# Masks by ScalarE, one product with U per batch, and u's transposes through one queue: a fused attention and low-rank mixing kernel on one core

## The chip, the core and the metric

The kernel runs on one core of a Trainium2 chip. The core has five engines that run in parallel, each with its own in-order queue and joined by semaphores: TensorE (PE in the profile; its weight loads are PEld), VectorE (DVE), ScalarE (ACT), GpSimd (POOL) and SyncE (SP), which here only issues transfers. PE writes to PSUM, where VectorE and ScalarE read its results. The metric is the time of one execution on the device in microseconds; a lower time is better. All times below are microseconds unless marked ns.

## The reference

Eight batches, eight heads, 576 positions, head width 64. Heads 0 to 3 attend locally (a position sees itself and the 31 before it), heads 4 to 7 in strides of 32. Then a mixing step over positions of rank 32, and a two-layer channel network with a residual.

```
rel = pos[:, None] - pos[None, :]
mask_local = (rel >= 0) & (rel < 32)
mask_strided = (rel >= 0) & (pos[None, :] % 32 == pos[:, None] % 32)
scores = np.where(masks, q @ k.T / 8, -1e9)
attn = exp(scores - max); attn /= sum + 1e-9
x = concat over heads of attn @ v          # 8 x 576 x 512
h = x.T @ U @ V                            # U 576 x 32, V 32 x 576
u = x + h.T
out = u + relu(u @ w_ch1) @ w_ch2          # 512 -> 2048 -> 512
```

The two weights arrive as 64-bit floats and are turned into 32-bit parts on the core.

## The kernel before

The channel network makes up most of the work. It runs over blocks of 512 rows: block n (0 to 7) holds the first 512 positions of batch n, and block 8 the last 64 positions of all eight batches. Each block has 16 steps `fc`, one for each 128 of the 2048 hidden columns. `gemm1` (L648) is 12 matmuls into one PSUM bank `ph`: four pieces `dc` of u^T, each as three products of a high and a low part (`uh`, `ul`, and the weights' two parts). ScalarE makes the hidden value `gh` of it (L652), VectorE its low part `gl` (L653). `gemm2` (L665) is 12 matmuls into the two accumulators `acc`. The main loop at the end of the function issues `gemm1` of a step, then `gemm2` of the step before. At the end of a block, `finish` adds the accumulator to u (L672) and sends it out, and `split` (L637) makes `uh` and `ul` of the next block from `raw`, which holds u^T.

The attention of a batch runs beside the block before its own. `attention(b)` is a generator; `advance` runs a number of its steps in each of the 32 slots of a block, two slots per step of the network, by the triple `A_EARLY` (block 0), `A_LATE` (blocks 1 to 6) or `A_TAIL`: first slot, last slot, number of steps. Its order for batches 2 to 7:

- `local_pairs`: two pairs of local heads. Per pair: PSUM tile `px` is taken (`psx2`; there is one, of two banks, and every stage below takes it in turn); two matmuls with an identity write the mask into it (L340, bfloat16, 320 columns for each head); 72 small matmuls add the scores (L346); VectorE takes the maximum and subtracts, ScalarE the exponential (L361); PE transposes (L368), ScalarE copies to `PT` (L371); 80 small matmuls with V (L381); VectorE normalises (L390 to L397).
- `mix_t`, first half of the columns, then the copies of the strided heads' result (`strided_copies`, L487 and L491), then `mix_t`, second half. `mix_t` is U^T x: four matmuls over four groups of 128 positions, each to its own 32 partitions (L514), four more for the last 64 positions (L518), whose results are added up by a copy on ScalarE (L523) and three adds on VectorE (L525), and made into three stacked parts `tst` (L527 to L529).
- `mix_u` and `mix_tail`: V's product (L537, L546) and its addition to x (L539, L552).
- `transposes`: VectorE transposes blocks of 32 by 32 into `bt` (L619), and 16 transfers per half, by SP and ScalarE in turn, move these into `raw`, in runs of 512 bytes.

The strided heads of batches 2 to 7 are done by GpSimd and VectorE without PE: `strided_heads` has GpSimd multiply (L442 for the scores, L470 for the values) and VectorE sum (L444, L472). `strided_upto` paces its 66 steps between the slots that `S0` and `S1` give, about from the middle of one block into the next.

Batches 0 and 1 are done by `first_attention`, ahead of the first block and into its first steps, with all their heads on PE; batch 1's mixing runs in block 0, with `attention(1)`, beside the conversion of the remaining weights (`to_f32` L129 to L132, `weights` L205 and L206).

The order of the instructions in each engine's queue is not the order in which the code writes them down. A scheduler takes it from a model of the times and from the order of the code as priority. `tc.issue_after(ins)` adds an edge: what the block writes comes behind `ins` in the queue of `ins`'s engine. `marks` collects instructions for such edges.

Of the kernel before, what the change touches and what calls it, by code (L numbers as in the profile page):

```python
# [17 lines left out]
NSP = 2  # L18
N_EARLY = 20
N_LATE = 48  # L20
N_STRIDED = 66
# [16 lines left out]
def fused_kernel(ctx, tc, pairs, strided, U, V, w_in, masks, eye, out):  # L38
    nc = tc.nc
    B, S, DM = out.shape  # L40
    D = 64
# [72 lines left out]
    zeros = raw.rearrange("p s a d x -> p (s a d x)")[:, 0:320].bitcast(BF16)  # L114
    nc.vector.memset(zeros, 0.0)
# [215 lines left out]

    def scores(kT, qT, mask):

        sp = psx2()
        done = marks.setdefault("scores", [])
        with tc.issue_after(done[-1]) if len(done) == 1 else nullcontext():
            for n in range(WARM.get(len(done), 0)):
                nc.tensor.matmul(sp[:, 0, :], zeros[:, 0:128], zeros[:, 128:640], start=True, stop=True, skip_group_check=True)
        for hh in range(2):
            nc.tensor.matmul(sp[:, hh, 0:320], ident_b, mask, start=True, stop=False, skip_group_check=True)  # L340
        for c in range(NCH):
            t, c4 = c // 4, c % 4
            k0 = max(0, 32 * c - 32)
            x0 = 64 * t + (0 if c else 32)
            for hh, rows in enumerate(halves):
                last = nc.tensor.matmul(sp[32 * c4:32 * c4 + 32, hh, x0:64 * t + 64], qT[rows, 32 * c:32 * c + 32],  # L346
                                        kT[rows, k0:32 * c + 32], start=False, stop=True, skip_group_check=True,
                                        tile_position=(64 * hh, 32 * c4))
        done.append(last.ins)
        return sp[:, :, 0:320].rearrange("p h (t x) -> p h t x", x=64)  # L350
# [23 lines left out]
    def outputs(PT, vt):  # L374

        op = psx2()
        for c in range(NCH):
            t, c4 = c // 4, c % 4
            for o4 in (c4,) if t < 4 else (c4, c4 + 2):
                for hh, rows in enumerate(halves):  # L380
                    last = nc.tensor.matmul(op[32 * o4:32 * o4 + 32, hh, (D + 1) * t:(D + 1) * t + D + 1],  # L381
                                            PT[rows, 32 * c:32 * c + 32], vt[rows, c], start=True, stop=True,
                                            skip_group_check=True, tile_position=(64 * hh, 32 * o4))
        marks.setdefault("PV", []).append(last.ins)
        return op[:, :, 0:5 * (D + 1)].rearrange("p h (t x) -> p h t x", x=D + 1)
# [15 lines left out]
    def local_pairs(b):  # L401

        xg, xt = x_tiles(b)
        tb = 64 * (b % 2)
        for pr in range(2):
            kT, qT = load_qk(b, pr)
            vt = load_v(b, pr)
            for _ in range(2):
                yield
            sp = scores(kT, qT, mask_l)  # L410
            yield
            s_sb = yield from probabilities(sp)
            yield
            PT = transposed(s_sb)
            yield
            op = outputs(PT, vt)
            yield
            cs = slice(2 * pr * D, 2 * pr * D + 2 * D)
            normalised(op, xg[:, :, cs], xt[tb:tb + 64, cs], tb)
            yield  # L420

    def strided_heads(b):
# [15 lines left out]
        for i in range(NCH):  # L438
            for j0 in range(0, i + 1, 9):
                n = min(9, i + 1 - j0)  # L440
                tmp = att([128, 9, D], "tmp")
                nc.gpsimd.tensor_tensor(out=tmp[:, 0:n], in0=sk[:, j0:j0 + n], in1=sq[:, i:i + 1].broadcast_to([128, n, D]),  # L442
                                        op=ALU.mult)
                late.append(lambda tmp=tmp, n=n, i=i, j0=j0: nc.vector.tensor_reduce(  # L444
                    out=s_st[:, i, j0:j0 + n], in_=tmp[:, 0:n], axis=AX.X, op=ALU.add))
                flush(1)
                yield
# [17 lines left out]
        for i in range(NCH):  # L465
            step = D if i < 9 else D // 2
            for d0 in range(0, D, step):
# [3 lines left out]
                                        in1=s_st[:, i, 0:i + 1].broadcast_to([128, i + 1, step]), op=ALU.mult)  # L471
                late.append(lambda tv=tv, i=i, d0=d0, step=step: nc.vector.tensor_reduce(  # L472
                    out=o_st[:, i, d0:d0 + step], in_=tv.rearrange("p j d -> p d j"), axis=AX.X, op=ALU.add))
# [28 lines left out]

    def mix_t(b, half):

        xg, xt = x_tiles(b)
        tb = 64 * (b % 2)
        cs = slice(256 * half, 256 * half + 256)
        ps_a = psx1()[:, 0:256]
        if b not in tsts:
            tsts[b] = ap_.tile([96, DM], F32R, name="tst")  # L510
        tst = tsts[b]
        with tc.issue_after(marks["acc"][2 + half]) if b < NSP else nullcontext():
            for j in range(4):
                nc.tensor.matmul(ps_a[32 * j:32 * j + 32, :], U_sb[:, j, :], xg[:, j, cs], start=True, stop=False,  # L514
                                 skip_group_check=True, tile_position=(0, 32 * j))
        for j in range(4):
            part = slice(64 * j, 64 * j + 64)
            nc.tensor.matmul(ps_a[32 * j:32 * j + 32, part], U_sb[tb:tb + 64, 4, :],  # L518
                             xt[tb:tb + 64, 256 * half + 64 * j:256 * half + 64 * j + 64], start=False, stop=True,
                             skip_group_check=True, tile_position=(tb, 32 * j))  # L520
        yield
        ta = att([32, 256], "ta")
        nc.scalar.copy(out=ta, in_=ps_a[0:32, :])  # L523
        for j in range(1, 4):
            nc.vector.tensor_tensor(out=ta, in0=ps_a[32 * j:32 * j + 32, :], in1=ta, op=ALU.add)  # L525
        yield
        nc.scalar.copy(out=tst[0:32, cs], in_=ta)  # L527
        nc.scalar.copy(out=tst[64:96, cs], in_=ta)
        nc.vector.tensor_tensor(out=tst[32:64, cs], in0=ta, in1=tst[0:32, cs].bitcast(F32), op=ALU.subtract)  # L529
        yield  # L530
# [64 lines left out]
    def attention(b):  # L595
        if b >= NSP:
            yield from local_pairs(b)
            yield from mix_t(b, 0)
            yield "strided"
            yield from strided_copies(b)  # L600
            yield from mix_t(b, 1)
            yield
# [3 lines left out]
        else:  # L606
            yield from mix_tail(0)
            for half in range(2):
                yield from mix_t(b, half)
            yield from mix_u(b)  # L610
# [3 lines left out]
    def transposes(n):  # L614

        for t in (0, 2):
# [18 lines left out]
    def split(n):  # L635

        for dc in range(NDC):  # L637
            hi, lo = (u[:, dc, :].rearrange("p (s a x) -> p s a x", s=4, a=4) for u in (uh, ul))
            nc.scalar.copy(out=hi, in_=raw[:, :, :, dc, :])  # L639
            nc.vector.tensor_tensor(out=lo, in0=raw[:, :, :, dc, :], in1=hi.bitcast(F32), op=ALU.subtract)  # L640

    accs = {}

    def gemm1(fc, dcs=range(NDC)):
        ph = ps_h.tile([128, 512], F32, name="ph")
        for dc in dcs:
            for i, (part, ut) in enumerate(((0, uh), (0, ul), (1, uh))):
                nc.tensor.matmul(ph, w_parts[fc, 0][:, part, 128 * dc:128 * dc + 128], ut[:, dc, :],  # L648
                                 start=(dc == dcs[0] and i == 0), stop=(dc == dcs[-1] and i == 2))
        gh = mp.tile([128, 512], F32R, name="gh", bufs=2)  # L650
# [18 lines left out]
    def finish(n):  # L669
        for s in range(4):  # L670
            ot = xgs[n][:, s, :]
            nc.vector.tensor_tensor(out=ot, in0=accs[n][s // 2][:, s % 2, :], in1=ot, op=ALU.add)  # L672
            if n == B:
                for bb in range(2):
                    (od_dma if bb else dma)(out=out[2 * s + bb, 512:576, :], in_=ot[64 * bb:64 * bb + 64, :])
            else:
                dma(out=out[n, 128 * s:128 * s + 128, :], in_=ot)

    conv = weights()
# [57 lines left out]
    for step, (n, fc) in enumerate(steps):  # L737
        pend.append((n, fc) + (gemm1(fc, ORDER0) if step == 0 else gemm1(fc)))
        if fc == NFC - 1 and n + 1 < NB:
            split(n + 1)  # L740
        advance(2 * step)
# [86 lines left out]
```

## Time and profile before

| | |
|---|---|
| median of three runs | 927.82 (927.54 to 929.11) |
| the profiled execution | 928.37 |
| its span, first to last instruction | 926.1 |
| granted TensorE clock, mean | 0.991 |
| start of the first `gemm1` | 49.5 |
| DMA, mean over the span | 81 GB/s |

A row of the timeline gives the start, the duration, the engine, line and operation, what it writes and reads, the shape and how many like it follow on each other; in brackets stand the idle time before it and what ended it. A matmul's row lasts longer than the step to the next one, since matmuls overlap; the cost of one in a sequence is read from the starts. A row of the groups ends with the busy time, the mean in ns, and the idle time before. A row of the windows view gives a stretch, its length, the busy time of each engine asked for with its number of instructions, then the granted clock, the share of the DMA engines and GB/s. A row of the waits gives who waited for whom: sum, number, longest.

### The profile page before, as it was taken

The page shows a single profiled execution, that of the slowest core. Times are in us where ns is not written, and L with a number is a line of the kernel's source. Part 1 is how long each engine was busy: PE and PEld are TensorE (multiplying, and loading weights), DVE is VectorE, ACT ScalarE, POOL GpSimd, SP SyncE. Part 2 cuts the span into 40 slices and gives each one's busy share as a digit, 9 for nine tenths or more (in the row PEclk, how much of TensorE's full clock was granted, in tenths as well). Part 3 has the DMA queues.
Part 4 walks back from the last instruction along what each step waited for, and adds up shares of the span by engine and source line. Part 5 has one row for each costly group of instructions (what it writes and reads, how often), then busy time and mean ns, then how long its engine had stood idle before and what let it go on. Part 6 is the DMA issues. An engine that isn't in the chain of part 4 may idle for free.

```text
span 926.1 us, 16819 instructions
## 1 busy us (share of the span) xinstructions
PE 902.6 (97%) x6997; PEld 718.0 (78%) x6998; DVE 548.6 (59%) x895; ACT 244.2 (26%) x478; POOL 338.4 (37%) x378
## 2 busy tenths in 40 slices
PE   7899989999999999999999999999999999999997
PEld 4667767777887788778877787778877888888885
DVE  4579996665886588658765786667863341122111
ACT  3457522142123312331224121422142111121110
POOL 1223493343853393429433764356530000000000
PEclk9899999999999999999999999999999999999999
DMA  9869313201230125011500141014200230001001
GB/s 352 299 205 357 117 54 107 73 2 52 76 145 2 52 55 178 1 52 33 181 8 18 50 168 50 1 53 148 73 1 1 57 120 17 1 1 46 0 1 46
DMA packets 39036, 75.29 MB, mean 81 GB/s; under 512 B 6464, under 2 KB 22864, under 8 KB 37040
## 3 DMA queue, kind: packets, MB, share of 16 engines
q1 hardware_dynamic: 27312, 66.87, 20.7%
q10 hardware_dynamic: 10560, 4.73, 2.0%
q0 software_dynamic: 1088, 2.62, 0.8%
q8 instruction: 55, 0.90, 0.4%
q14 instruction: 21, 0.17, 0.1%
HBM read 54.14 MB, written 11.67 MB: 71 GB/s over the span
## 4 chain that ended last, share of the span: by engine, by line
PE 84%; DVE 4%; DMA 2%; POOL 1%; issue 1%; ACT 0%; SPq 0%; DVEq 0%; ACTq 0%; POOLq 0%
PE acc L665 40%; PE ph L648 39%; PE px L381 1%; DMA w<-in_w_dram 1%; PE px L346 1%; DVE cv L132 1%; DVE s_st L444 1%; PE px L368 1%; PE px L514 1%; DMA od<-x 1%; PE px L537 1%; DMA st<-in_strided_dram 1%; DVE w L206 1%; POOL tmp L442 1%; DVE gl L653 0%
## 5 line engine op out<-in xcount | busy, mean ns | idle before, releaser
L653 DVE SCALAR_TENSOR_TENSOR gl<-ph,gh 128x512 fp32r<-128x512 f32 x144 | 98.9, 688 | 230.1 <-ACT gh L652 229.4
L648 PE MATMUL ph<-uh,w 128*128 128x512 f32 x648 | 215.9, 394 | 0.0
L652 ACT ACTIVATE gh<-ph 128x512 fp32r<-128x512 f32 x144 | 86.2, 599 | 476.9 <-PE ph L648 400.8
L470 POOL TENSOR_TENSOR tmp<-st,s_st 128x448 f32<-128x448 f32 (+7 forms) x162 | 137.3, 876 | 190.8 <-DVE st L472 106.8
L442 POOL TENSOR_TENSOR tmp<-st 128x576 f32<-128x576 f32 (+6 forms) x162 | 175.0, 1121 | 76.5 <-DMA st<-in_strided_dram 66.6
L665 PE MATMUL acc<-w,gh 128*128 128x512 f32 x648 | 196.8, 391 | 0.0
L648 PEld LDWEIGHTS ph<-uh,w 128*128 128x128 f32 x648 | 121.9, 189 | 26.8
L665 PEld LDWEIGHTS acc<-w,gh 128*128 128x128 f32 x648 | 121.3, 188 | 25.6
L472 DVE TENSOR_REDUCE st<-tmp 128x64 f32<-128x64 f32 (+8 forms) x162 | 136.3, 878 | 7.8 <-POOL tmp L470 7.0
L648 PE MATMUL ph<-ul,w 128*128 128x512 f32 x324 | 126.8, 391 | 0.0
L665 PE MATMUL acc<-w,gl 128*128 128x512 f32 x324 | 121.6, 392 | 4.1 <-DVE gl L653 4.1
L444 DVE TENSOR_REDUCE s_st<-tmp 128x9 f32<-128x576 f32 (+6 forms) x162 | 87.2, 563 | 17.5 <-POOL tmp L442 16.7
L665 PEld LDWEIGHTS acc<-w,gl 128*128 128x128 f32 x324 | 61.0, 188 | 18.4 <-DVE gl L653 5.2
L648 PEld LDWEIGHTS ph<-ul,w 128*128 128x128 f32 x324 | 61.1, 189 | 12.6
L487 ACT COPY xg<-st 32x256 f32<-32x256 f32 x96 | 38.8, 404 | 9.1 <-DVE st L472 7.7
L525 DVE TENSOR_TENSOR ta<-px,ta 32x256 f32<-32x256 f32 x42 | 17.6, 420 | 36.5 <-ACT ta L523 35.6
L672 DVE TENSOR_TENSOR xg<-acc,xg 128x512 f32<-128x512 f32 x36 | 22.9, 682 | 13.4 <-PE acc L665 13.4
L539 DVE TENSOR_TENSOR xg<-px,xg 128x512 f32<-128x512 f32 x28 | 18.0, 684 | 11.9 <-PE px L537 11.9
L648 PE MATMUL ph<-uh,w6a 128*128 128x512 f32 x72 | 24.3, 398 | 0.0
L640 DVE TENSOR_TENSOR ul<-raw,uh 128x512 fp32r<-128x512 f32 x32 | 21.1, 682 | 5.3 <-ACT uh L639 5.3
L648 PE MATMUL ph<-uh,w1a 128*128 128x512 f32 x72 | 23.9, 391 | 0.0
L648 PE MATMUL ph<-uh,w2a 128*128 128x512 f32 x72 | 23.9, 391 | 0.0
(265 smaller groups left out, 1252.9 us busy)
## 6 DMA issues: line engine op xcount, KB each, us to landing
w<-in_w_dram SPq DMA_DIRECT2D x9, 1024.0 KB, 13.3
out_dram<-xg SPq DMA_DIRECT2D x32, 256.0 KB, 2.1
v<-in_pairs_dram SPq DMA_DIRECT2D x12, 585.0 KB, 5.1
st<-in_strided_dram SPq DMA_DIRECT2D x6, 1152.0 KB, 5.4
qk<-in_pairs_dram SPq DMA_DIRECT2D x12, 576.0 KB, 5.1
late<-in_pairs_dram SPq DMA_DIRECT2D x8, 585.0 KB, 8.3
late<-in_pairs_dram SPq DMA_DIRECT2D x8, 576.0 KB, 8.1
raw<-bt SPq DMA_DIRECT2D x128, 32.0 KB, 1.9
```

The source lines that it names most:

```text
L442: nc.gpsimd.tensor_tensor(out=tmp[:, 0:n], in0=sk[:, j0:j0 + n], in1=sq[:, i:i + 1].broadcast_to([128, n, D]), op=ALU.mult)
L444: late.append(lambda tmp=tmp, n=n, i=i, j0=j0: nc.vector.tensor_reduce(out=s_st[:, i, j0:j0 + n], in_=tmp[:, 0:n], axis=AX.X, op=ALU.add))
L470: nc.gpsimd.tensor_tensor(out=tv, in0=sv[:, 0:i + 1, d0:d0 + step], in1=s_st[:, i, 0:i + 1].broadcast_to([128, i + 1, step]), op=ALU.mult)
L472: late.append(lambda tv=tv, i=i, d0=d0, step=step: nc.vector.tensor_reduce(out=o_st[:, i, d0:d0 + step], in_=tv.rearrange("p j d -> p d j" ...
L487: nc.scalar.copy(out=xg[32 * i4:32 * i4 + 32, :, cs], in_=o_st[rows, i4:16:4, :])
L539: nc.vector.tensor_tensor(out=xg[:, t + s, :], in0=pv[:, s, :], in1=xg[:, t + s, :], op=ALU.add)
L640: nc.vector.tensor_tensor(out=lo, in0=raw[:, :, :, dc, :], in1=hi.bitcast(F32), op=ALU.subtract)
L648: nc.tensor.matmul(ph, w_parts[fc, 0][:, part, 128 * dc:128 * dc + 128], ut[:, dc, :], start=(dc == dcs[0] and i == 0), stop=(dc == dcs[-1 ...
L652: marks.setdefault("gh", []).append(nc.scalar.activation(out=gh, in_=ph, func=AF.Relu).ins)
L653: low = nc.vector.scalar_tensor_tensor(out=gl, in0=ph, scalar=0.0, in1=gh.bitcast(F32), op0=ALU.max, op1=ALU.subtract)
L665: last = nc.tensor.matmul(accs[n][s // 2][:, s % 2, :], gt[:, cs], w_parts[fc, 1][:, part, :], start=(fc == 0 and i == 0 and n > 0), stop= ...
L672: nc.vector.tensor_tensor(out=ot, in0=accs[n][s // 2][:, s % 2, :], in1=ot, op=ALU.add)
```

## The change

ScalarE writes the mask of the pairs of batches 2 to 7: it copies the mask for both heads into `px` one step ahead of the scores, which then come behind the `gemm1` last written. `outputs` sets PE's flag that starts a new accumulation in its first group of four chunks only, and the rest comes behind that. The early pairs keep their masks on PE. `mix_t` runs once per batch, over all 512 columns, behind the strided copies. The strided sums that VectorE makes are put behind the adds of the last `finish` written. `raw` changes its layout so that each partition gets 1 KB at a time, all transfers go through SP, and `split` takes each piece in two halves. At a block's first step, `gemm2` of the block before and `finish` are now written down ahead of the attention's steps. The pacing numbers change.

```diff
-N_EARLY = 20
-N_LATE = 48
+N_EARLY = 17
+N_LATE = 47
-A_LATE = (1, 28, N_LATE)
+A_LATE = (2, 26, N_LATE)
-S1 = (14, 14)
+S1 = (12, 12)
...
-    raw = const.tile([128, 4, 4, NDC, 32], F32, name="raw")
+    raw = const.tile([128, 2, 4, 2, NDC, 32], F32, name="raw")
...
+    def masked():
+        sp = psx2()
+        nc.scalar.copy(out=sp[:, :, 0:320], in_=mask_l.broadcast_to([128, 320, 2]).rearrange("p x h -> p h x"))
+        return sp
+
+    def scores(kT, qT, mask, sp=None):
+        if sp is None:
+            sp = psx2()
+            with_mask(sp, mask)
...
+            with tc.issue_after(first) if t else nullcontext():
...
+                                                PT[rows, 32 * c:32 * c + 32], vt[rows, c], start=t == 0, stop=True,
...
-            sp = scores(kT, qT, mask_l)
+            sp = masked()
+            yield
+            with tc.issue_after(marks["ph"][-1]):
+                sp = scores(kT, qT, mask_l, sp)
...
+    def reduced(**what):
+        with tc.issue_after(marks["out"][-1]) if "out" in marks else nullcontext():
+            nc.vector.tensor_reduce(**what)
...
-    def mix_t(b, half):
+    def mix_t(b):
...
-                nc.tensor.matmul(ps_a[32 * j:32 * j + 32, :], U_sb[:, j, :], xg[:, j, cs], start=True, stop=False,
+                nc.tensor.matmul(ps_a[32 * j:32 * j + 32, :], U_sb[:, j, :], xg[:, j, :], start=True, stop=False,
...
-            part = slice(64 * j, 64 * j + 64)
+            part = slice(128 * j, 128 * j + 128)
...
-        ta = att([32, 256], "ta")
+        ta = att([32, 512], "ta")
...
             yield from local_pairs(b)
-            yield from mix_t(b, 0)
             yield "strided"
             yield from strided_copies(b)
-            yield from mix_t(b, 1)
+            yield from mix_t(b)
...
-                    (od_dma if q % 2 else dma)(out=raw[32 * q:32 * q + 32, t:t + 2, a].rearrange("p s d x -> p s (d x)"),
-                                               in_=bt[32 * a:32 * a + 32, q].rearrange("p s d x -> p s (d x)"))
+                    dma(out=raw[32 * q:32 * q + 32, t // 2, a].rearrange("p s d x -> p (s d x)"),
+                        in_=bt[32 * a:32 * a + 32, q].rearrange("p s d x -> p (s d x)"))
...
-            hi, lo = (u[:, dc, :].rearrange("p (s a x) -> p s a x", s=4, a=4) for u in (uh, ul))
-            nc.scalar.copy(out=hi, in_=raw[:, :, :, dc, :])
-            nc.vector.tensor_tensor(out=lo, in0=raw[:, :, :, dc, :], in1=hi.bitcast(F32), op=ALU.subtract)
+            for t in range(2):
+                hi, lo = (u[:, dc, 256 * t:256 * t + 256].rearrange("p (s a x) -> p a s x", s=2, a=4) for u in (uh, ul))
+                nc.scalar.copy(out=hi, in_=raw[:, t, :, :, dc, :])
+                nc.vector.tensor_tensor(out=lo, in0=raw[:, t, :, :, dc, :], in1=hi.bitcast(F32), op=ALU.subtract)
...
+        ends = len(pend) > 1 and pend[0][1] == NFC - 1
+        if not ends:
+            advance(2 * step)
         if n == 0:
             convert(2 * upto[min(NFC - 1, fc + CLA)])
         if len(pend) > 1:
-            item = pend.pop(0)
-            gemm2(*item)
-            if item[1] == NFC - 1:
-                finish(item[0])
+            gemm2(*pend.pop(0))
+        if ends:
+            finish(n - 1)
+            advance(2 * step)
         advance(2 * step + 1)
```

More of the change, by code (lines that the diff above doesn't have):

```diff
@@ L330, in od_reads, with with_mask @@
             far_dma(out=xt[tb + 32 * i4:tb + 32 * i4 + 32, 256:512], in_=ov[16 + i4])
-    def scores(kT, qT, mask):
-        sp = psx2()
+    def with_mask(sp, mask):
         done = marks.setdefault("scores", [])
@@ L376, in outputs @@
         op = psx2()
+        first = None
         for c in range(NCH):
             t, c4 = c // 4, c % 4
[L379 to L383, printed above, removed]
+            with tc.issue_after(first) if t else nullcontext():
+                for o4 in (c4,) if t < 4 else (c4, c4 + 2):
+                    for hh, rows in enumerate(halves):
+                        last = nc.tensor.matmul(op[32 * o4:32 * o4 + 32, hh, (D + 1) * t:(D + 1) * t + D + 1],
+                                                PT[rows, 32 * c:32 * c + 32], vt[rows, c], start=t == 0, stop=True,
+                                                skip_group_check=True, tile_position=(64 * hh, 32 * o4))
+            if t == 0:
+                first = last.ins
         marks.setdefault("PV", []).append(last.ins)
@@ L501, in x_tiles @@
         return xgs[b], tails[b // 2]
-    def mix_t(b, half):
+    def mix_t(b):
         xg, xt = x_tiles(b)
         tb = 64 * (b % 2)
[L507 to L512, printed above, removed]
+        ps_a = psx1()
+        tst = tsts[b] = ap_.tile([96, DM], F32R, name="tst")
+        with tc.issue_after(marks["acc"][3]) if b < NSP else nullcontext():
             for j in range(4):
-                nc.tensor.matmul(ps_a[32 * j:32 * j + 32, :], U_sb[:, j, :], xg[:, j, cs], start=True, stop=False,
+                nc.tensor.matmul(ps_a[32 * j:32 * j + 32, :], U_sb[:, j, :], xg[:, j, :], start=True, stop=False,
                                  skip_group_check=True, tile_position=(0, 32 * j))
         for j in range(4):
-            part = slice(64 * j, 64 * j + 64)
-            nc.tensor.matmul(ps_a[32 * j:32 * j + 32, part], U_sb[tb:tb + 64, 4, :],
-                             xt[tb:tb + 64, 256 * half + 64 * j:256 * half + 64 * j + 64], start=False, stop=True,
-                             skip_group_check=True, tile_position=(tb, 32 * j))
+            part = slice(128 * j, 128 * j + 128)
+            nc.tensor.matmul(ps_a[32 * j:32 * j + 32, part], U_sb[tb:tb + 64, 4, :], xt[tb:tb + 64, part],
+                             start=False, stop=True, skip_group_check=True, tile_position=(tb, 32 * j))
         yield
-        ta = att([32, 256], "ta")
+        ta = att([32, 512], "ta")
         nc.scalar.copy(out=ta, in_=ps_a[0:32, :])
@@ L607, in attention @@
             yield from mix_tail(0)
-            for half in range(2):
-                yield from mix_t(b, half)
+            yield from mix_t(b)
             yield from mix_u(b)
@@ L647, in gemm1 @@
             for i, (part, ut) in enumerate(((0, uh), (0, ul), (1, uh))):
-                nc.tensor.matmul(ph, w_parts[fc, 0][:, part, 128 * dc:128 * dc + 128], ut[:, dc, :],
-                                 start=(dc == dcs[0] and i == 0), stop=(dc == dcs[-1] and i == 2))
+                last = nc.tensor.matmul(ph, w_parts[fc, 0][:, part, 128 * dc:128 * dc + 128], ut[:, dc, :],
+                                        start=(dc == dcs[0] and i == 0), stop=(dc == dcs[-1] and i == 2))
+        marks.setdefault("ph", []).append(last.ins)
         gh = mp.tile([128, 512], F32R, name="gh", bufs=2)
@@ L671, in finish @@
             ot = xgs[n][:, s, :]
-            nc.vector.tensor_tensor(out=ot, in0=accs[n][s // 2][:, s % 2, :], in1=ot, op=ALU.add)
+            last = nc.vector.tensor_tensor(out=ot, in0=accs[n][s // 2][:, s % 2, :], in1=ot, op=ALU.add)
             if n == B:
@@ L677, in finish @@
                 dma(out=out[n, 128 * s:128 * s + 128, :], in_=ot)
+        marks.setdefault("out", []).append(last.ins)
     conv = weights()
```

14 lines of the change are left out of this document (7 added, 7 removed).

## The prediction, made before the changed kernel was run

> **What bounds it now.** I read the page's busy times first, then the windows view of stretches inside the run, then the waits of TensorE (PE). All times are microseconds.
>
> ```profile
> span 926.1 us, 16819 instructions
> PE 902.6 (97%) x6997; PEld 718.0 (78%) x6998; DVE 548.6 (59%) x895; ACT 244.2 (26%) x478; POOL 338.4 (37%) x378
> ```
> ```profile
> sum 389.36, PE 389.36; mean PE 97.34
> ...
> 163.60:919.50 755.90, 755.90 (x5152) 1.00 0.16 53
> ```
> ```profile
> PE acc L665 <- DVE gl L653: 4.1, 3, 1.9
> ```
>
> The first windows row is the sum of four stretches of 97.34 from 261.0 on, each one block long: PE is busy for all of each. The second says the same of everything from 163.6 to 919.5, at the full clock (1.00). So from there on nothing that PE waits for can be shortened, because it waits for nothing; only instructions taken off PE shorten the span, one for one, and anything else done faster by another engine is worth nothing. The last row is the waits view from 57.0 to 139.5, in block 0: three waits, 4.1 together, for VectorE's low part `gl`. That is the only place where another engine ends the wait. So I price two things: what leaves PE after 139.5, and what happens to the stall of block 0.
>
> **Masks.** In the timeline of PE a mask pair (L340) stands alone ahead of `gemm2`, or directly ahead of the scores (L346).
>
> ```profile
> 442.43 0.39 PE L648 MATMUL ph<-uh,w 128*128 128x512 f32 x1
> 442.66 0.45 PE L340 MATMUL px<-masks_sb 128*128 128x320 bf16 x2
> 442.83 1.19 PE L665 MATMUL acc<-w,gh 128*128 128x512 f32 x4
> ...
> 448.39 1.07 PE L665 MATMUL acc<-w,gh 128*128 128x512 f32 x4
> ```
> ```profile
> 361.71 0.39 PE L648 MATMUL ph<-uh,w1a 128*128 128x512 f32 x1
> 362.03 0.92 PE L346 MATMUL px<-qk 64*32 64x32 f32 x72
> ...
> 382.77 0.39 PE L665 MATMUL acc<-w3b,gh 128*128 128x512 f32 x1
> ...
> 383.38 0.92 PE L346 MATMUL px<-qk 64*32 64x32 f32 x72
> ```
>
> Four undisturbed matmuls take 1.07, so their starts lie (1.07 - 0.39)/3 = 0.227 apart. With a mask between, 442.43 to 442.83 is 0.40, that is 0.17 more, and the next four take 1.19, 0.12 more: 0.29. Ahead of scores: from the last GEMM start to the scores 0.61 with masks (382.77 to 383.38) against 0.32 without (361.71 to 362.03): 0.29 again. There are 12 such pairs (batches 2 to 7, two each); the first stands just before the stall of block 0 ends and gives nothing. 11 x 0.29 = **3.2**.
>
> What replaces them is a ScalarE copy of 640 elements per partition. The nearest row has that size; the second is the release that it waits for, VectorE's last read of the bank in pair 0:
>
> ```profile
> L361 ACT ACTIVATE s_sb<-s_sb 128x640 f32<-128x640 f32 x12 | 8.9, 741 | 39.3 <-DVE s_sb L357 39.3
> ```
> ```profile
> 378.90 0.27 DVE L397 TENSOR_TENSOR xt<-px,rt 64x128 f32<-64x128 f32 x1
> ```
>
> So 12 x 0.74 = 8.9 more on an engine that is busy 26%: nothing, while it is covered. The cover: the bank is free at 379.17, a copy would end at about 379.9, and the scores start at 383.38, 3.5 later. The new wait is PE's for ScalarE; behind the scores on PE stands the whole GEMM, behind the copy on ScalarE stands the next `gh`. If the cover is gone, each microsecond of lateness costs PE one in each of 12 pairs (a rival below).
>
> **U's products.** Before, two inserts per batch, of 256 columns; after, one of 512.
>
> ```profile
> 404.80 0.39 PE L648 MATMUL ph<-ul,w 128*128 128x512 f32 x1
> 405.11 0.64 PE L514 MATMUL px<-xg,U_sb 128*32 128x256 f32 x8
> 405.68 0.32 PE L518 MATMUL px<-xt,U_sb 64*32 64x64 f32 x8
> 405.93 0.73 PE L648 MATMUL ph<-uh,w 128*128 128x512 f32 x2
> ```
> ```profile
> L514 PE MATMUL px<-xg,U_sb 128*32 128x256 f32 x112 | 8.9, 391 | 0.0
> L518 PE MATMUL px<-xt,U_sb 64*32 64x64 f32 x112 | 4.4, 228 | 0.0
> ```
>
> An insert costs 405.93 - 404.80 - 0.227 = 0.90, and 0.11 after it (two matmuls in 0.73; undisturbed 0.227 + 0.39 = 0.62): 1.01, 2.02 a batch. The eight matmuls are four, in two passes (the four of a pass overlap). Per column and pass (391 - 228)/192 = 0.85 ns. Doubling both widths adds 2 x (256 + 64) x 0.85 ns = 0.54, so one wide insert costs 1.55 and a batch saves 0.47. The ends: nothing, if an insert's cost is all width; 1.01, if it is all switching. I take 0.47, since the rows give both shares. Batches 2 to 7 run after 139.5: 6 x 0.47 = **2.8** (0 to 6). Batch 1's lies ahead of the stall and is swallowed by it. The copies and adds behind it double in width and halve in number, beside PE.
>
> **Scores in pieces.** In block 1, batch 2's first scores were started early and cut into five pieces between GEMM matmuls; the first, the fourth with its neighbours, and the last:
>
> ```profile
> 145.06 0.37 PE L346 MATMUL px<-qk 64*32 64x32 f32 x20
> ...
> 159.62 0.61 PE L648 MATMUL ph<-uh,w0a 128*128 128x512 f32 x2
> 160.17 0.31 PE L346 MATMUL px<-qk 64*32 64x64 f32 x6
> 160.41 0.50 PE L648 MATMUL ph<-ul,w0a 128*128 128x512 f32 x1
> ...
> 167.90 0.44 PE L346 MATMUL px<-qk 64*32 64x64 f32 x28
> ```
>
> The second of the two at 159.62 starts at 159.85; to 160.41 it is 0.56, 0.33 too much, and 0.11 more follows (0.50 for 0.39): 0.44. Six matmuls themselves take 6 x 0.012 = 0.07 (72 in 362.03 to 362.88), so a cut costs 0.37. The new order edge puts the scores behind the `gemm1` last issued when they are written down, which in this block is after its first steps, so they come in one piece: four cuts less, **1.4** (0 to 1.5). That their end moves is nothing: the last piece ended as late as that.
>
> **Transfers and split.** Last rows of a block, SP, ScalarE's queue, ScalarE, PE:
>
> ```profile
> 409.62 0.34 SPq L96 DMA_DIRECT2D st<-in_strided_dram  x1
> 429.14 12.67 SPq L96 DMA_DIRECT2D raw<-bt  x16
> ```
> ```profile
> 437.25 5.50 ACTq L99 DMA_DIRECT2D raw<-bt  x8
> ...
> 449.45 2.17 ACT L639 CAST uh<-raw 128x512 fp32r<-128x512 f32 x4
> ```
> ```profile
> 452.02 0.39 PE L648 MATMUL ph<-uh,w0a 128*128 128x512 f32 x1
> ```
> ```profile
> raw<-bt SPq DMA_DIRECT2D x128, 32.0 KB, 1.9
> ```
>
> ScalarE's last eight issues take 5.50, 0.69 each; a plain one on SP takes 0.34. So 16 on SP take 5.4 to 11 a half; of the two I stand nearer the lower, as the runs get plain: 7. Both halves from 429.14 then end at 443.2 (451.1 at the worst) and land 1.9 later, 445.1 (453.0). The split began at 449.45, held by `gemm1`'s reads of `uh`, and PE needed its first piece at 452.02. Covered by 4 to the split and 7 to PE; at the worst PE is 1 late. I cost it at nothing. SP was through at 429.14 + 12.67 = 441.81, now at 443.2: what is queued behind on SP (the strided heads' V, then K, Q and V of the next batch) comes 1.4 later, and the next block's scores run at 362.03 + 97.34 = 459.37. Eight half pieces for four whole ones cost ScalarE and VectorE at most double, 4.3 for 2.17; they end by 453.8, and PE takes them one quarter of `gemm1` after the other. ScalarE loses 16 issues a block, 11, and wins nothing by it, since `gh` was not waited for.
>
> **Order of sums.** Sums behind the four adds (L672) start later in each block. Behind them on VectorE stands `gl`, behind the sums GpSimd's next product, behind those the batch's copies and U's products:
>
> ```profile
> 408.55 1.05 ACT L491 COPY xt<-st 32x64 f32<-32x64 f32 x4
> ...
> 416.98 0.36 ACT L523 COPY ta<-px 32x256 f32<-32x256 f32 x1 [3.04 <-PE px L518]
> ```
>
> The last copy ends at 409.60, the second half's sum is taken up at 416.98: about 6 of cover for some 3 of delay. Nothing.
>
> **Block 0's stall.**
>
> ```profile
> 120.00:139.30 19.30, 19.21 (x26) 0.91 0.24 71
> ```
> ```profile
> 91.56 1.20 DVE L206 TENSOR_TENSOR w<-cv,w 128x1024 fp32r<-128x1024 f32 x1
> ```
> ```profile
> L444 DVE TENSOR_REDUCE s_st<-tmp 128x9 f32<-128x576 f32 (+8 forms) x21 | 10.6, 523 | 1.1 <-POOL tmp L442 1.0
> ...
> L206 DVE TENSOR_TENSOR w<-cv,w 128x1024 fp32r<-128x1024 f32 x5 | 8.3, 1663 | 0.0
> ...
> L525 DVE TENSOR_TENSOR ta<-px,ta 32x256 f32<-32x256 f32 x3 | 1.3, 420 | 0.1
> ```
>
> VectorE is busy 19.21 of 19.30, and the groups from 100 to 139.3 show what with. Beside GpSimd's products a conversion (L206) takes 1.66, alone 1.20. The change takes the second half's three adds and one subtraction (1.3 + 0.4) out of this stretch, as the single product comes earlier in the pacing, and brings in two sums (2 x 0.52): the strided heads have 22 slots in place of 24 (`S1`), so at the end of the block 29 of 65 parts are due, not 27. Net 0.7 less VectorE work, which the stall gives back: **0.7**, between 5.8 (all of it: 4.1 waited, and 0.09 of 19.3 lost to the clock, 1.7) and -4.
>
> **Sum.** 3.2 + 2.8 + 1.4 + 0.7 = 8.1. The profiled execution took 928.37, its span and 2.3 around it, and comes to 920.3; the median of the three runs is 0.55 lower, 927.82, so 919.7.
>
> **Rivals.** *The stall of block 0 goes altogether*: for it, 0.7 fewer microseconds in an engine that is exactly full, and ScalarE free of 16 issues there; against, two more sums. 919.7 + 0.7 - 5.8 = 914.6.
>
> *The stall grows*: VectorE is full, and GpSimd's products, drawn ahead by `S1`, slow its conversions. By the rows 5 x 0.46 = 2.3 lost on L206 beside 21 parts, and as much on L132 if it suffers alike: 0.22 a part. Two parts more: 1.5 with their sums, no adds gained, and another 1.7 of slow clock: 919.7 + 0.7 + 1.5 + 1.7 = 923.6. [...]
>
> *The inserts are no cheaper*: the wide U product costs twice the narrow one and the scores are cut as before. 919.7 + 2.8 + 1.4 = 923.9.
>
> *PE waits for ScalarE's masks* (the other side). ScalarE takes its queue in order; if VectorE's release or a copy queued ahead holds the mask up by more than the 3.5 of cover, PE stands at the scores with the GEMM behind them. At 4.5 late it is 1 in each of 12 pairs, 931.7 with the rest as forecast; 0.85 in each is where it becomes slower. Against it: PT and the exponential, also ScalarE's, stand ahead of PE in each pair now, and PE waits for neither after 163.6.
>
> **Chances.** Forecast 0.60, own range 917 to 922; stall gone 0.12; stall grown 0.12; inserts no cheaper 0.09; PE waits 0.07. The range leaves out the last and the far ends of the second and third: 913.5 to 925.5. A measurement of this kernel tells 0.2%, 1.9, from no change: faster 0.87, within it 0.07, slower 0.06.
>
> **What would show it.** Block length 97.34 falls to 96.3 (two masks, one insert: 0.58 + 0.47), with PE busy throughout; no L340 after the first attention; L514 at about 0.6 per matmul, x56 with twice the columns; L346 of batch 2 in one run of 72; the waits of PE after block 0 empty. I am wrong if PE waits at L346 for ScalarE, at L648 for VectorE's `ul`, or if the wait for `gl` in block 0 is not between 2 and 5.

## The result and the profile after

| | before | changed |
|---|---|---|
| median, runs on the same chip | 928.47 (927.54 to 930.70, 4 runs) | 917.62 (916.81 to 919.74, 4 runs) |
| ratio of the two | | 0.9883, 95% interval 0.9858 to 0.9909 |
| the profiled execution | 928.37 | 918.08 |
| its span | 926.1 | 916.0 |
| granted TensorE clock, mean | 0.991 | 0.993 |
| first `gemm1` | 49.5 | 48.8 |

The change is worth 10.85 in the medians and 10.3 in the profiled executions; 8.1 was forecast. The changed kernel's page, busy times, and two rows of its groups by shape:

```profile
span 916.0 us, 16587 instructions
...
PE 893.4 (98%) x6862; PEld 714.1 (78%) x6862; DVE 548.3 (60%) x899; ACT 253.2 (28%) x501; POOL 339.4 (37%) x378
```
```profile
L536 PE MATMUL px<-xg,U_sb 128*32 128x512 f32 x56 | 7.5, 605 | 0.0
```
```profile
L343 ACT CAST px<-masks_sb 128x640 f32<-128x640 bf16 x12 | 8.4, 698 | 1.9 <-DVE xt L573 1.8
```

PE gives up 9.2 of busy time, ScalarE takes 9.0 more, 8.4 of it the masks. Next the windows view over blocks 2 to 5, as in the prediction:

```profile
252.80:349.10 96.30, 96.30 (x721) 1.00 0.19 61
349.10:446.00 96.90, 96.61 (x721) 1.00 0.22 71
446.00:542.20 96.20, 96.20 (x720) 1.00 0.21 68
542.20:639.10 96.90, 96.61 (x721) 1.00 0.20 67
sum 386.30, PE 385.71; mean PE 96.43
```

389.36 before, 386.30 now: 0.77 a block, where 1.05 was forecast. Two of the four blocks are 96.2 or 96.3, the forecast figure, and two are 96.9; in these PE no longer is busy for all of the block. The waits of PE, first from 57 to 140, then from 140 to 915, say why:

```profile
PE acc L686 <- DVE gl L674: 4.2, 4, 1.6
```
```profile
PE acc L686 <- ACT gh L673: 0.6, 2, 0.3
```

The stall of block 0 is still there (4.1 before). And there is a new wait behind the start of blocks 3 and 5, short and only there. The place in the timeline of PE:

```profile
349.08 0.39 PE L668 MATMUL ph<-uh,w0a 128*128 128x512 f32 x1
349.31 0.39 PE L668 MATMUL ph<-uh,w1a 128*128 128x512 f32 x1
...
354.98 1.19 PE L686 MATMUL acc<-w0b,gh 128*128 128x512 f32 x4 [0.29 <-ACT gh L673]
```

`gemm1` of the block's first two steps (w0a and w1a) take turns, so both end together and `gemm2` finds no `gh`: 354.98 - 354.30 - 0.227 = 0.46 each time, and the slower matmuls behind it make 0.57 of it. It is the order in PE's queue that counts: in blocks 3 and 5 two matmuls of the second step stand between the first step's last one and `gemm2`, in blocks 2, 4 and 6, which have no wait, five.

To see where the 10 went I took the starts of the network's matmuls in both traces. In a run without disturbance they lie 0.227 apart; what is more than that (differences below 0.02 left out) I put down to what stands between the two.

| part of the span | before | changed | difference |
|---|---|---|---|
| start to the first `gemm1` | 49.51 | 48.75 | -0.76 |
| from there to 100, excess | 15.02 | 13.78 | -1.24 |
| 100 to 140 (the stall), excess | 8.27 | 6.49 | -1.78 |
| after 140: masks and scores | 14.82 | 11.30 | -3.52 |
| after 140: U's products | 10.88 | 8.64 | -2.24 |
| after 140: gaps between network matmuls | 6.26 | 5.74 | -0.52 |
| after 140: all other inserts | 28.68 | 28.70 | 0.02 |

The sum is -10.04, 0.1 from the difference of the spans. The gaps hold the slow matmuls behind an insert, 0.11 each time, which go with the insert, and the new wait, which is added: 0.55 less for the masks, 0.44 less for pieces of scores, 0.66 less for U, 1.13 more for the wait. That gives -0.52, all of the row.

### The profile page after: what moved, and what is told of

It is laid out like the page before. It is cut to its first block, busy times and chain, and to the rows that moved or that the text cites. A ratio compares the mean times of both kernels' runs of the same rounds, so it can differ in the third digit from the quotient of the medians.

```text
span 916.0 us, 16587 instructions
## 1 busy us (share of the span) xinstructions
PE 893.4 (98%) x6862; PEld 714.1 (78%) x6862; DVE 548.3 (60%) x899; ACT 253.2 (28%) x501; POOL 339.4 (37%) x378
## 4 chain that ended last, share of the span: by engine, by line
PE 84%; DVE 4%; DMA 2%; POOL 1%; issue 1%; ACT 1%; SPq 0%; DVEq 0%; POOLq 0%; ACTq 0%
PE acc L686 40%; PE ph L668 39%; PE px L397 1%; DMA w<-in_w_dram 1%; PE px L357 1%; PE px L379 1%; DVE s_st L445 1%; PE px L536 1%; PE px L558 1%; DVE cv L132 1%; DMA st<-in_strided_dram 1%; DVE w L206 1%; DMA od<-x 1%; DVE gl L674 0%; POOL tmp L467 0%
## 5 line engine op out<-in xcount | busy, mean ns | idle before, releaser
L467 POOL TENSOR_TENSOR tmp<-st 128x576 f32<-128x576 f32 (+6 forms) x162 | 177.0, 1128 | 127.6 <-DMA st<-in_strided_dram 71.7
L660 DVE TENSOR_TENSOR ul<-raw,uh 128x256 fp32r<-128x256 f32 x64 | 25.4, 432 | 12.9 <-ACT uh L659 12.5
L693 DVE TENSOR_TENSOR xg<-acc,xg 128x512 f32<-128x512 f32 x36 | 22.7, 682 | 17.4 <-PE acc L686 17.4
L659 ACT CAST uh<-raw 128x256 fp32r<-128x256 f32 x64 | 23.2, 404 | 19.5 <-DMA raw<-bt 10.2
L668 PE MATMUL ph<-uh,w0a 128*128 128x512 f32 x72 | 24.1, 391 | 0.0
## 6 DMA issues: line engine op xcount, KB each, us to landing
w<-in_w_dram SPq DMA_DIRECT2D x9, 1024.0 KB, 13.3
```

The costliest lines, as they stand in the source:

```text
L659: nc.scalar.copy(out=hi, in_=raw[:, t, :, :, dc, :])
L660: nc.vector.tensor_tensor(out=lo, in0=raw[:, t, :, :, dc, :], in1=hi.bitcast(F32), op=ALU.subtract)
L668: last = nc.tensor.matmul(ph, w_parts[fc, 0][:, part, 128 * dc:128 * dc + 128], ut[:, dc, :], start=(dc == dcs[0] and i == 0), stop=(dc == ...
L693: last = nc.vector.tensor_tensor(out=ot, in0=accs[n][s // 2][:, s % 2, :], in1=ot, op=ALU.add)
```

## The experiments

All kernels compute all of the reference. The kernel before ran beside each set; its medians there were 928.76, 929.34, 928.73 and 928.91, so times of different sets compare to within about one.

| run | edit to the changed kernel | median | ratio to before (95%) |
|---|---|---|---|
| e1 | masks back on PE | 920.79 | 0.9911 (0.9887 to 0.9934) |
| e2 | U's product in two halves, both behind the copies | 937.26 | 1.0081 (1.0055 to 1.0107) |
| e3 | no edge for the scores | 923.84 | 0.9945 (0.9924 to 0.9965) |
| e4 | kernel before, with the new start flags of `outputs` | 928.45 | 0.9992 (0.9975 to 1.0009) |
| e5 | u^T's transfers by SP and ScalarE in turns | 938.50 | 1.0097 (1.0071 to 1.0124) |
| e6 | e2 and e5 together | 968.98 | 1.0430 (1.0411 to 1.0450) |
| e7 | no edge for the sums | 921.89 | 0.9925 (0.9908 to 0.9942) |
| e8 | `S1` of the kernel before | 918.59 | 0.9888 (0.9870 to 0.9907) |
| e9 | attention paced one slot earlier | 922.16 | 0.9926 (0.9904 to 0.9948) |
| e10 | attention paced two slots later | 932.24 | 1.0037 (1.0022 to 1.0051) |
| e11 | e2, paced two slots earlier | 930.84 | 1.0030 (1.0010 to 1.0049) |
| e12 | transfers, split and pacing of the kernel before | 924.55 | 0.9950 (0.9936 to 0.9965) |

### The terms of the sum: e1, e3, e4

Masks back on PE (e1):

```diff
-            sp = masked()
+            sp = psx2()
+            with_mask(sp, mask_l)
```

> The changed kernel, but PE writes the masks of the pairs of batches 2 to 7 again (two matmuls with the identity where ScalarE's copy stood). Theory, PE is full after block 0 and each mask pair costs it 0.29: 11 or 12 x 0.29 = 3.2 to 3.5 more than the changed kernel, 920.8 to 921.1, block length 0.58 longer. Rival, the gain came from block 0 and the transfers, and masks were hidden: within 1 of 917.6, blocks of the same length.

920.79 against 917.62: 3.2 slower, the price forecast for the masks. In the trace, masks stand again in six inserts with the scores and in five alone, and cost 3.15 after 140. But the new wait of the changed kernel is gone in this run (PE waits for nothing after 140), so the stretch after 140 is only 2.3 longer, and the rest of the 3.2 lies ahead of it. That the medians differ by just the price is in part luck; the trace shows the price, and the ratios to the kernel before put the whole at 2.6.

The scores without their edge (e3):

```diff
-            with tc.issue_after(marks["ph"][-1]):
-                sp = scores(kT, qT, mask_l, sp)
+            sp = scores(kT, qT, mask_l, sp)
```

> The changed kernel without the edge that puts a pair's scores behind the gemm1 last written. Theory, without it scores that are ready early are cut up again between GEMM matmuls, 0.37 a cut: at least the four cuts of batch 2, 1.4 more, 919.0, and more if other pairs are cut too. Rival, ScalarE's mask one step ahead already keeps them together: 917.6 and runs of 72.

6.2 slower. The timeline of PE in this kernel, block 2:

```profile
260.17 0.43 PE L357 MATMUL px<-qk 64*32 64x32 f32 x26
260.54 1.20 PE L685 MATMUL acc<-w0b,gh 128*128 128x512 f32 x4
```

The scores stand in 25 pieces instead of 12, in blocks where the kernel before had none cut: the excess under scores rises from 11.30 to 14.40, the gaps from 5.74 to 7.21, together 4.6. So the edge is worth more inside the changed kernel than the one cut batch of the kernel before. Why the later scores stayed whole there without it was not settled.

The start flags alone, put into the kernel before (e4; the core of the edit):

```diff
-                    last = nc.tensor.matmul(op[...], PT[rows, 32 * c:32 * c + 32], vt[rows, c], start=True, stop=True,
+                    last = nc.tensor.matmul(op[...], PT[rows, 32 * c:32 * c + 32], vt[rows, c], start=t == 0, stop=True,
```

> The kernel before with one part of the change alone: the start flag of the products with V in the first group only, and the order edge in outputs. The queues' order is the same as before, so only the flags differ. Theory, the 2.0 that the changed kernel is earlier up to 100 are waits of PE for its own instructions (issue) and vary from run to run: within 1.5 of the kernel before, about 928, with issue waits of PE up to 100 anywhere between 3 and 6. Rival, the flags make the products with V cheaper: 2 less, 926, and issue waits near 3.2 as in the changed kernel.

No difference. The run is also a measure of what comes by itself: its first `gemm1` stands at 47.6 against 49.5, and PE waits 6.4 for `gl` in block 0 against 4.1.

### The miss: U's product in two halves (e2)

```diff
-            yield from mix_t(b)
+            yield from mix_t(b, 0)
+            yield from mix_t(b, 1)
```

with the widths of before in `mix_t`, and `N_EARLY` and `N_LATE` three steps up.

> The changed kernel, but the product with U in two halves of 256 columns, both behind the strided copies, with the numbers of steps made longer by three. Theory: two inserts of 1.01 for one of 1.55, 0.47 a batch in blocks 1 to 6, so 2.8 more, 920.4. Rival, the cost goes by width alone: 0, 917.6. In block 0 the stall may move by 1 either way.

937.26: 17 more than the expectation. The inserts cost what was worked out (10.88 in all after 140, against 8.64), and scores in 21 pieces add 2.5; but the gaps grow by 13.3. Of these, 1.65 go with 15 more inserts, and most of the rest is waits. Waits of PE after 140, then SP's and ScalarE's timeline ahead of block 3, which starts at 354.41:

```profile
PE ph L674 <- DVE ul L666: 7.6, 6, 1.8
```
```profile
342.22 10.01 SPq L96 DMA_DIRECT2D raw<-bt  x16
```
```profile
353.58 1.33 ACT L665 CAST uh<-raw 128x256 fp32r<-128x256 f32 x4 [2.88 <-DMA raw<-bt]
```

PE stands at the start of the block for `ul`. SP issues the second half from 342.22 to 352.23, the last piece lands, and only at 353.58 does ScalarE begin to split it. So a longer chain in front of the transposes is paid for at the block's start. Two causes are possible: the transfers, issued one after the other by SP, or the chain itself. The next runs try both.

### SP's serial issues: e5 and e6

```diff
-                    dma(out=raw[32 * q:32 * q + 32, t // 2, a].rearrange("p s d x -> p (s d x)"),
+                    (od_dma if q % 2 else dma)(out=raw[32 * q:32 * q + 32, t // 2, a].rearrange("p s d x -> p (s d x)"),
```

in the changed kernel (e5), and in the kernel of e2 (e6).

> The changed kernel with u^T's 1 KB transfers issued by SyncE and ScalarE in turns instead of by SyncE alone. Theory A, the new wait of about 0.46 us x 2 at block starts comes from SyncE's serial issues (16 of 0.64 us, some 10 us a half): each half takes about 5 us of either queue, the second half's first cast on ScalarE stands 4 to 5 us earlier than 2.2 us before the block's start, gemm1 of a block's first two steps are no longer interleaved, the two waits for gh go, and the time is 916.7 (0.9 under the changed kernel). Theory B, the wait has another cause, and ScalarE now issues beside its casts and copies: 917.6, or up to 1.5 more if its 64 issues a block delay gh.

> The kernel of the miss (U's product in two halves, 937.3) with u^T's transfers on two queues as in the run beside it. Theory A, the miss came from the transfers: the longer chain starts the transposes later, SyncE's 20 us of serial issues then end after the block's start, and PE waits for uh and ul. With some 10 us taken off, the waits for ul go and the time is what the inserts alone give, 917.6 + 2.9 = 920.5, at most 923. Theory B, it came from the longer chain itself (one more accumulator's round trip, 21 pieces of scores in place of 12): the time stays over 933.

938.50, 21 slower than the changed kernel: a miss for A in the time, and B has the kind but not the size. What A says of the data did come: a half's issues are shorter, and the two waits for `gh` are gone. ScalarE's timeline, then PE's, then the waits of PE after 140:

```profile
322.42 0.60 ACT L673 ACTIVATE gh<-ph 128x512 fp32r<-128x512 f32 x1 [5.33 <-PE ph L668]
325.64 5.96 ACTq L99 DMA_DIRECT2D raw<-bt  x8
331.70 0.60 ACT L673 ACTIVATE gh<-ph 128x512 fp32r<-128x512 f32 x1 [8.68 <-DMA raw<-bt]
```
```profile
333.81 1.09 PE L686 MATMUL acc<-w,gh 128*128 128x512 f32 x4
338.04 0.50 PE L686 MATMUL acc<-w,gl 128*128 128x512 f32 x1 [3.14 <-DVE gl L674]
```
```profile
PE acc L686 <- DVE gl L674: 13.9, 5, 3.1
```

Eight issues take 5 to 6 on ScalarE, and a step of the network takes 24 x 0.227 = 5.4. Where they start just behind a `gh` they fit between two steps; here they start 3.2 behind one, the next `gh` comes 9.3 after the last instead of 5.4, `gl` comes after it, and PE stands. The five waits are 13.9 of the 21; most of the rest is the clock, which falls to half behind three of them, for 13.6 in all. The longest such stretch:

```profile
639.11:645.93 6.82, 5.90 (x14) 0.50 0.61 198
```

There 14 matmuls are busy for 5.90, 0.42 each instead of 0.227. PE is busy for 12.7 of the 13.6, and at half clock that costs about half, 6. In e6 sixteen stand in a row (11.5), the clock is at half for 6.8 in each of five blocks, and it is 968.98. So e6 doesn't tell e2's two causes apart: the price of ScalarE's queue hides both. What it does tell: in the forecast, taking 16 issues a block off ScalarE was put at nothing, "since `gh` was not waited for". In the kernel before the issues fell beside the `gh`s (one of them, a `gh`, then seven); in this order they cost 21.

### Cover at the block's start: e9, e10, e11

```diff
-A_LATE = (2, 26, N_LATE)
+A_LATE = (2, 25, N_LATE)
```

28 in e10; 24 with the two halves of e2 in e11.

> The changed kernel with the next batch's attention paced to end one half step earlier in a block (25 in place of 26 of 32, about 3 us). Theory A, the two waits for gh at block starts (0.9 us) come from u^T's second half, whose first cast stands only 2.2 us before the block's start: 3 us more cover takes them away, and the time is 916.7, within 1, as long as the inserts stay one piece. Theory B, the chain of strided sums, copies, U's product and V's products sets the transfers, not the pacing: 917.6 and the same casts, or slower where a fuller half step leaves PE waiting in the middle of a block.

> The changed kernel paced to end two half steps later (28, the figure of the kernel before; about 6 us). Theory A, the cover at a block's start is 2 to 3 us: SyncE's second sixteen transfers end some 3 us behind the block's start, PE waits for uh and ul at 6 block starts for 2 to 4 us each, and the time is 930 to 942. Theory B, cover is left, since gemm2 of the last step and the first half's part of the split fill the gap: 917 to 920.

> The kernel of the first miss (U's product in two halves, all transfers by SyncE, 937.3), paced two half steps earlier (24, about 6 us), with nothing else changed. Theory A, its miss was the late second half of u^T at each block's start: the waits for ul go and what stays is the price of the six inserts and of scores in more pieces, 920.5 to 924. Theory B, the longer chain costs by itself, wherever it stands: over 933.

One slot earlier (e9): SP, ScalarE and PE.

```profile
333.23 10.87 SPq L96 DMA_DIRECT2D raw<-bt  x17
```
```profile
345.16 1.62 ACT L659 CAST uh<-raw 128x256 fp32r<-128x256 f32 x5
```
```profile
258.35 0.36 PE L357 MATMUL px<-qk 64*32 64x32 f32 x18
258.64 1.20 PE L686 MATMUL acc<-w0b,gh 128*128 128x512 f32 x4
```

The five casts run without a pause and PE waits for nothing after 140: the new wait is gone, as theory A has it. But scores are cut again, 24 pieces for 12, 3.3 more; it is 922.16. The pacing that keeps the scores whole and the one that leaves cover are not the same.

Two slots later (e10): SP, PE, and the waits of PE.

```profile
339.18 10.86 SPq L96 DMA_DIRECT2D raw<-bt  x17
```
```profile
351.84 0.50 PE L668 MATMUL ph<-uh,w0a 128*128 128x512 f32 x1 [0.83 <-ACT uh L659]
...
353.01 0.50 PE L668 MATMUL ph<-ul,w0a 128*128 128x512 f32 x1 [0.44 <-DVE ul L660]
```
```profile
PE ph L668 <- DVE ul L660: 5.9, 6, 1.6
PE acc L686 <- ACT gh L673: 1.7, 6, 0.3
PE ph L668 <- ACT uh L659: 1.2, 2, 0.8
PE acc L686 <- DVE gl L674: 0.9, 1, 0.9
```

932.24, theory A in kind and in the total, though a single wait for `ul` is 1.6 at most, under the 2 to 4 expected. In e11 the waits of PE after 140:

```profile
PE ph L674 <- DVE ul L666: 5.2, 6, 1.6
```

930.84, between the two theories. The waits for `ul` remain, because the transfers hardly moved (SP issues the second half up to 351.98, 2.7 before the start of block 3, in e2 2.2): with two products the chain in front of the transposes, not the pacing, sets them. Put side by side, the end of SP's second half before the start of block 3, and PE's listed waits from the start of block 2 on:

| kernel | SP's end to block's start | waits |
|---|---|---|
| before (two queues) | 8.5 | none |
| e9 | 349.85 - 344.10 = 5.7 | none |
| e1 | 3.8 | none |
| changed | 349.08 - 345.58 = 3.5 | 0.6 |
| e8 | 3.5 | 0.6 |
| e7 | 3.3 | 0.6 |
| e11 | 2.7 | 5.2 |
| e3 | 2.4 | 0.7 |
| e2 | 2.2 | 8.3 |
| e10 | 351.84 - 350.04 = 1.8 | 9.7 |

Block 3 alone doesn't order the kernels, since the blocks differ (in e3 four of the six starts from block 2 on have 4.6 or more). Over the starts of blocks 2 to 7 of the nine kernels with SP alone it is plain: each of the 22 with at most 3.6 has a wait behind it, three of the five from 3.8 to 4.4, and none of the 27 from 4.5 up. The changed kernel stands at the edge. So e2's miss lies at the block's start, and the link is the end of SP's second half. In e2, e10 and e11 PE stands for `ul` itself; in the changed kernel it stands for `gh`, because of the order of its queue, and that the scheduler chose this order for the later transfers fits e5 and e9, where order and wait are both gone, but isn't shown.

### The rest of the order: e7, e8, e12

No edge for the sums (e7): `with tc.issue_after(marks["out"][-1])` in `reduced` becomes `with nullcontext()`.

> The changed kernel without the rule that puts the strided sums behind a block's adds. Theory A, the order of these sums is worth nothing, as the forecast had it: 917.6, within 1. Theory B, the sums stand ahead of the adds at a block's end on VectorE, accumulators come free later and PE waits at a block's start: some 0.5 to 1.2 us at each of 8 ends, 921 to 927.

4.3 slower, in theory B's range, but its kind at one end of a block only. The waits of PE from 140 to 200, then from 200 on:

```profile
PE ph L668 <- DVE ul L660: 1.5, 2, 1.1
PE acc L686 <- DVE xg L693: 0.6, 2, 0.4
```
```profile
PE acc L686 <- ACT gh L673: 0.6, 2, 0.3
```

The last row is the changed kernel's own. The others stand at the end of block 0: there VectorE takes ten sums from 151.28 to 164.08, between the subtractions of the split and ahead of the adds (L693), where the changed kernel takes none from 149.73 to 161.58. At the start of block 3 the two kernels' adds and sums have the same order. These waits and their slow matmuls make 3.6 after 140 (58.01 against 54.37); the rest lies in the first 100 and isn't explained, so that the time falls into B's range is partly luck.

Sums spread as before (e8): `S1 = (14, 14)`.

> The changed kernel with the strided products and sums of each batch spread over 14 steps instead of 12. Theory A, what is left of the stall in block 0 (four waits for gl, 4.9 us with that for xt) is VectorE's density there: fewer sums a step, and 1 to 3 us of it go, 915 to 917. Theory B, the waits come from the order of conversions and adds round the end of the first attention, not from the sums: 917.6, or up to 3 more, since the strided batch ends later and what hangs on it starts later.

Theory B: 918.59, the wait for `gl` in block 0 is 3.9 against 4.2. How densely the sums are paced is worth nothing here.

Transfers, split and pacing undone (e12; the edit is the change's own lines for these, reversed).

> The changed kernel with u^T's transfers, raw's layout, the split by whole tiles and the pacing (1 to 28) of the kernel before; the masks on ScalarE, U's product in one piece and both rules of order stay. Theory A, the forecast's, that the transfers' part is worth nothing by itself: masks, inserts and whole scores keep their 7.4 us and the new wait of 0.9 at block starts is gone, 916 to 918. Theory B, the transfers' part is needed with the rest: eight issues of 0.6 us each on ScalarE stand ahead of a gh that is ready, as in the run with two queues (13.9 us of waits for gl, 938.5), and PE waits for it once or twice a block: 925 to 938.

924.55: neither. PE waits for nothing after 140, against theory B: here ScalarE's eight issues start right behind a `gh` and just fit. But A's figure is missed by 7. ScalarE:

```profile
331.03 0.60 ACT L672 ACTIVATE gh<-ph 128x512 fp32r<-128x512 f32 x1 [5.30 <-PE ph L667]
331.09 6.05 ACTq L99 DMA_DIRECT2D raw<-bt  x8
337.25 0.60 ACT L672 ACTIVATE gh<-ph 128x512 fp32r<-128x512 f32 x1 [5.62 <-DMA raw<-bt]
```

The scores are in 29 pieces in spite of their edge, 4.7 more; the rest lies in the first 100, where this execution has a stretch at half clock (0.96 from 57 to 140). So the package of transfers, split and pacing is worth some 5 after the start, by whole scores and not by earlier data. Which part of it keeps them whole stays open: with the new transfers they are whole at 26 and at 28 (e10) and cut at 25 (e9). Transfers by SP and GpSimd in turns were not tried, and neither the split in halves nor the new order at a block's first step was undone by itself, so no run prices them.

## Right and wrong, step by step

- **Masks: 3.2 forecast**; 3.15 in the trace (2.60 in the inserts, 0.55 behind them), and again in e1's. The cover was put at 3.5. ScalarE and PE, changed kernel:

```profile
380.86 0.70 ACT L343 CAST px<-masks_sb 128x640 f32<-128x640 bf16 x1
```
```profile
383.23 0.61 PE L668 MATMUL ph<-uh,w6a 128*128 128x512 f32 x2
383.78 0.92 PE L357 MATMUL px<-qk 64*32 64x32 f32 x72
```

  The copy ends at 381.56, the scores start at 383.78: 2.2, less than forecast as four strided copies stand ahead of it. The rival in which PE waits for ScalarE's masks did not come; no wait of PE is at L357. The gap ahead of the scores is 383.78 - 383.46 = 0.32, as worked out.
- **U's products: 2.8 forecast**; 2.90 in the trace. The wide insert:

```profile
404.76 0.39 PE L668 MATMUL ph<-uh,w 128*128 128x512 f32 x1
405.08 1.06 PE L536 MATMUL px<-xg,U_sb 128*32 128x512 f32 x8
406.07 0.42 PE L540 MATMUL px<-xt,U_sb 64*32 64x128 f32 x8
406.42 0.73 PE L686 MATMUL acc<-w,gh 128*128 128x512 f32 x2
```

  406.42 - 404.76 - 0.227 + 0.11 = 1.54; 1.55 was forecast from two narrow shapes. Batch 1's saving (0.37) was not swallowed by the stall, though the prediction says so: the waits for `gl` there are 4.2 against 4.1. e2 bears the price out in the trace (10.88 in the inserts against 8.64), though its time came out another way.
- **Pieces of scores: 1.4 forecast**; 1.36 (0.92 and 0.44 behind them). Right, but e3, e9 and e12 show that it is the most sensitive step: the forecast asked only what the edge repairs, not what the new order would cut without it.
- **Transfers and split: nothing forecast, with 7 a half and cover of 4 and 7.** The step that failed in size. SP and ScalarE in the changed kernel:

```profile
334.69 10.89 SPq L96 DMA_DIRECT2D raw<-bt  x17
```
```profile
346.94 1.33 ACT L659 CAST uh<-raw 128x256 fp32r<-128x256 f32 x4 [2.15 <-DMA raw<-bt]
```

  17 in 10.89 is 0.64 each, near ScalarE's 0.69 in the row that the prediction quoted and not near the plain 0.34 it leaned to: 16 take 10.2. It cost 1.1 by the new wait, where the prediction expected no wait of PE after block 0. Of the cover of 7 forecast for PE, 1.7 to 3.7 was left at blocks 2 to 7: SP's end stands 3.5 to 5.5 ahead of them, and a transfer lands 1.8 after its issue. The issues are the larger part here: sixteen take 10.2 and one landing 1.8. In e5 the time saved on SP is paid for by the engine it is moved to: eight issues take ScalarE 5 to 6, and a `gh` behind them comes 9.3 after the last instead of 5.4.
- **Order of sums: nothing forecast**, between the kernel before and the changed one. In the changed kernel the edge is worth 4.3 in the medians (e7) and 3.6 after 140, nearly all of it at the end of block 0, where the split's subtractions and the adds share VectorE with ten sums that would stand ahead of them. The prediction looked for what the edge delays and not for what would be late without it.
- **Block 0's stall: 0.7 forecast, by VectorE's work; the mechanism failed.** The waits are the same (4.2 against 4.1), and e8 shows that two sums more or less don't matter. VectorE's work did not fall: it is busy 19.20 of 19.30 from 120 on, 19.21 before. The adds left, but two more block transposes came in (100 to 139.3, before and changed), which the forecast didn't count:

```profile
L619 DVE STREAM_TRANSPOSE bt<-xg 128x512 f32<-128x512 f32 x2 | 1.3, 680 | 0.0
```
```profile
L638 DVE STREAM_TRANSPOSE bt<-xg 128x512 f32<-128x512 f32 x4 | 2.6, 684 | 0.0
```

  What changed is the clock. Windows from 57 to 140, before and changed:

```profile
57.00:140.00 83.00, 77.00 (x596) 0.98 0.46 170
```
```profile
57.00:140.00 83.00, 77.61 (x565) 1.00 0.46 167
```

  0.02 x 83 = 1.7, and 1.78 is what 100 to 140 gained. The prediction had this 1.7 in its range, but only together with the waits. One reading in it is off: the 1.66 for a conversion beside GpSimd's products is a mean over five, of which two came before these products (1.22 and 1.20) and three beside them, which run from 105.81 to 137.50 (1.70, 2.26, 1.93); the 2.3 lost in all stands.
- **The first 100: nothing forecast, 2.0 gained.** Of it 0.37 is batch 1's product; the rest is in waits that the profile puts down to PE's issue (5.1 before, 3.2 changed) and in the start. e4, whose PE does the same as before's, moves by 1.9 in the start alone. I take this part for the spread between executions; it isn't shown.

In sum 3.15 + 2.90 + 1.36 + 1.78 - 1.13 + 2.0 = 10.1, for 8.1 forecast: the three terms that the rows priced came out within 0.1 each, and the rest were errors of either sign. The 1.1 more in block 0 and the 1.1 lost at block starts cancelled, and 2.0 that isn't explained stayed: that the total lies in the stated range is in part luck, that the three terms came out is not. No rival came as written.

## What to carry to other kernels

Once PE waits for nothing, price an edit by the start-to-start distances around each insert: it was right to 0.1 here. Then ask of every freed or moved queue how far its last item now stands from its deadline, since a term of "nothing, covered" was where the costly misses lay (SP's end 3.5 before a block, eight issues in a step of 5.4). And an order that a scheduler happened to give (whole scores, issues right behind a `gh`) can go with one slot of pacing, so count the pieces in the trace after each edit, whatever it was meant to do.

## What the runs showed of the hardware

- Stretches at half clock stood behind short waits of PE. Among the runs whose longest wait for `gl` in block 0 was 1.8 or less, the granted clock from 100 to 140 was 1.00 in all nine; with a longest wait of 1.9 or 2.9 it was 0.96 or 0.97 in four of five (before, e4, e6, e11; not e2): half clock for 3.4. That is no threshold: in e2 half clock from 456.54 to 459.95 began 0.18 behind the end of a single wait of 1.79, three other waits of 1.5 in that run cost no clock, and in e5 half clock followed three of the four waits of 3.0 and 3.1.

```profile
456.54:459.95 3.41, 3.41 (x9) 0.50 0.89 254
```

  Waits of 1.8 to 3.1 with work around them went ahead of these stretches; why of some waits and not of others like them isn't shown.
- One issue of a 32 KB transfer of 32 partitions takes SP 0.64 in a row of them, about twice the 0.34 of the plain load quoted in the prediction.
